# Two integers spread by VectorE's shuffle instead of a matrix product, and one product moved forward at the end

## The chip, the cores and the metric

The kernel runs on one core of a Trainium2 chip. The metric is the device time of one execution in microseconds (us). A profiled execution has a span of its own, from its first instruction to its last.

## What is computed

An attention over 2 batches, 8 heads, 768 positions and 64 channels per head, with a window of `n_local` positions and `n_global` global keys, is followed by two feed-forward layers (512 to 2048 to 512) over the 1536 rows.

```python
scores = scale * np.matmul(q, k.transpose(0, 1, 3, 2))
keep = is_global | is_local            # pos < n_global ; 0 <= rel < n_local
dist = np.where(is_global & ~is_local, float(n_local), np.abs(rel))
scores = np.where(keep, scores - slopes * dist, -1e9)
a = softmax(scores)
x = np.matmul(a, v)                    # rows x 512
h = x @ w_in;  g = np.maximum(0.01 * h, h);  x = g @ w_out
h = x @ w2_in; g = P(h) / (Q(h) + 1e-6);     out = g @ w2_out
```

`n_local` and `n_global` are 64-bit integers in device memory. The kernel reads them at run time; the mask and the bias of the attention are made from them.

## The kernel before

**Number form.** Every large product is made of three TensorE products of split numbers: a high part times a high part, and the two cross terms (names end in h and l: `qh`, `ql`, `kh`, `kl`, `gh`, `gl`).

**Start.** SP's queue loads q and k of the first pair of heads (`qr`, `kr`, half 0 before half 1), then k of pair 1, v and q of pair 1. SP's first issue for half 1 of k waits until the first DMA of ACT's queue has landed, since both use one completion counter. ACT's queue loads the two integers into one partition (`ints`, L95 and L96) and then one of the four first pieces of k (L300). VectorE makes positions and distances (L236 to L241) and turns the integers into floats in one partition (`read_ints`, L105 to L109). They are needed in all 128 partitions, as `nums`. For that TensorE multiplies a row of ones by them (L500, tile `spread`), and VectorE copies the result (L509). Then VectorE makes the bias: `bias_far` (L245, L248), `bias_near` (L251), `bias_half` (L254).

TensorE's own order is written out by hand. `keep_busy(n)` (L489) issues n dummy products that nobody reads. The start is 14 dummies, the spreading product, 1 dummy, then the transposes of `qr` and `kr` (L331), 3 dummies, and the first scores (L402). `prep_q` and `prep_k` work on the transposes: `qh` on ACT (L370), `kh` on ACT (L341), `ql` on VectorE (L372), `kl` on VectorE (L343). VectorE's queue holds the bias ahead of `ql`, so `ql` and `kl`, and with them the scores that read `kl`, start after the bias is made.

**Middle.** 96 units of attention go by in a hand-made order, and transposes of the next pairs are issued between them by the slots in `PREP0` and `PREP`. Then 96 units of the two layers follow: for each, `h` (L675), an activation into `gh` and `gl`, and the products into the four banks `y` (`emit_y`, L796 and L798). Each unit adds three products to each bank.

**End.** `emit_ends` writes out the last two units. Unit u-1 is the last one, and its activation comes in two halves: half 0 serves banks 0 and 1, half 1 serves banks 2 and 3. ACT makes the high part (`hi`, L910), VectorE the low part (`lo`, L913). TensorE gets the products of unit u-2 for banks 0 and 1, those of unit u-1 for banks 0 and 1, then for bank 2 and for bank 3 first u-2 and then u-1. `ys[d]()` copies bank d out and stores it (L814 or L816, L818).

Of the kernel before, what the change touches and what calls it, by code (L numbers as in the profile page):

```python
# [8 lines left out]
F32 = mybir.dt.float32  # L9
F32R = mybir.dt.float32r  # L10
I32 = mybir.dt.int32
U32 = mybir.dt.uint32
AF = mybir.ActivationFunctionType
ALU = mybir.AluOpType
# [3 lines left out]
P = 128  # L18
# [8 lines left out]
def attention_moe_moe2(  # L27
# [15 lines left out]
    nc = tc.nc  # L43
# [7 lines left out]
    NK = DM // P  # L51
# [9 lines left out]
    LOAD_Q = 5  # L61
    XOUT = (8, 9)

    BUSY = (14, 1, 3, 2, 1, 2)

    FIRST = 8
    XOUT_LAST = (1, 8)
# [17 lines left out]
    RUN_AHEAD = 2  # L85

    W2 = 2 * P
    BW = W2 + P

    cpool = ctx.enter_context(tc.tile_pool(name="cpool", bufs=1))  # L90
    xpool = ctx.enter_context(tc.tile_pool(name="xpool", bufs=1))


    ints = cpool.tile([1, 4], I32, name="ints")
    nc.scalar.dma_start(ints[:, 0:2], n_local.bitcast(I32).partition_broadcast(1))  # L95
    nc.scalar.dma_start(ints[:, 2:4], n_global.bitcast(I32).partition_broadcast(1))  # L96
    intf = cpool.tile([1, 4], F32, name="intf")
    num1 = cpool.tile([1, 2], F32, name="num1")
    warm = cpool.tile([P, P], F32R, name="warm")
    ones = warm.bitcast(F32)[0:1]  # L100
    nums = cpool.tile([P, 2], F32, name="nums")
    n_loc = nums[:, 0:1]
    n_glo = nums[:, 1:2]

    def read_ints():  # L105
        nc.vector.tensor_copy(intf, ints)
        lo, hi = (intf.rearrange("p (j w) -> p j w", w=2)[:, :, w] for w in range(2))
        nc.vector.scalar_tensor_tensor(hi, lo, 0.0, hi, ALU.is_lt, ALU.add)
        nc.vector.scalar_tensor_tensor(num1, hi, 4294967296.0, lo, ALU.mult, ALU.add)  # L109

    coef = cpool.tile([P, 8], F32, name="coef")

# [110 lines left out]
    def window_bias(bpool, rpool):  # L223
# [3 lines left out]
        misc2 = rpool.tile([P, 2 * DM], F32, tag="raw", name="misc2")  # L227
        rel_i = misc[:, 0:BW]
        dist = misc.bitcast(F32)[:, BW : 2 * BW]
        mask = misc2[:, 0:BW]  # L230
        nc.gpsimd.iota(rel_i[:, 0:W2], [[-1, W2]], base=P, channel_multiplier=1)
        nc.gpsimd.iota(rel_i[:, W2:BW], [[-1, P]], base=0, channel_multiplier=1)
        col_i = bpool.tile([P, GW], I32, name="col_i")
# [10 lines left out]
        def far():  # L244
            nc.vector.tensor_scalar(mask, dist, n_loc, FAR, ALU.is_ge, ALU.mult)  # L245
            mask_g = misc2[:, 0 : 2 * W2].rearrange("p (a c) -> p a c", a=2)[:, :, 0:GW]
            col_g = col.unsqueeze(1).to_broadcast([P, 2, GW])
# [10 lines left out]
    def attention(wpool, w1, ffn):  # L258
        with ExitStack() as actx:
# [4 lines left out]
            ps = actx.enter_context(tc.tile_pool(name="ps", bufs=2, space=PSUM))  # L264
# [4 lines left out]
            def blocks(t, s):  # L269

                if s == 0:
                    return t[:, 0 : HB * W2].rearrange("p (i c) -> p i c", c=W2)[:, :, 0:P]
                c0 = HB * W2 - P
                return t[:, c0 : c0 + HB * W2].rearrange("p (i c) -> p i c", c=W2)[:, :, P:W2]
# [212 lines left out]
            def keep_busy(n, rows=P):  # L487
                for _ in range(n):
                    nc.tensor.matmul(  # L489
                        idle[:, 0:W2].rearrange("p (a c) -> p a c", a=2),  # L490
                        warm[0:rows],
                        warm[0:rows].unsqueeze(1).to_broadcast([rows, 2, P]),
                        start=True,
                        stop=True,
                    )

            bias, bias_far, bias_near, bias_half = window_bias(bpool, rpool)
            keep_busy(BUSY[0])
            spread = ps.tile([P, W2], F32, tag="pt", name="spread")[:, 0:2]
            nc.tensor.matmul(spread, ones, num1, start=True, stop=True)  # L500
            keep_busy(BUSY[1])
            q0, k0, q1, k1 = P_[0].prep_q(0), P_[0].prep_k(0), P_[0].prep_q(1), P_[0].prep_k(1)
            next(q0)
            next(k0)
            next(q0)
            next(k0)
            keep_busy(BUSY[2])
            own, rest = slice(W2, BW), slice(0, W2)
            nc.vector.tensor_copy(nums, spread)  # L509
            bias_far()  # L510
            bias_near(own)
            next(q0, None)
# [91 lines left out]
            def unit(n):  # L604
                return U[n] if 0 <= n < len(U) else None
# [8 lines left out]
            n = 0  # L614
            while n < len(U) or running or n <= len(U) + LV + 1:

                for m in GROUPS.get(n, ()):
                    for step, _ in enumerate(zip(unit(m).scores(), unit(m + 1).scores())):
                        if n == 0 and step == 0:
                            keep_busy(BUSY[3], P // 2)  # L620
                    if m == 2:
                        for _ in zip(unit(4).scores(), unit(5).scores()):
                            pass
                        keep_busy(BUSY[4])
                for m in LEASTS.get(n, ()):
                    unit(m).least()
                    if m == 1:
                        bias_near(rest)
                        bias_half(rest)
                if unit(n - 1) and n != 3:  # L630
                    unit(n - 1).exp()
                if unit(n - 3):
                    unit(n - 3).transposes()
                    if n == 4:
                        keep_busy(BUSY[5], P // 2)
                    unit(n - 3).evacuate()
                if n == 3:
                    unit(2).exp()
                for m in {LV: (), LV + 1: (0, 1)}.get(n, (n - LV,)):
                    if unit(m):  # L640
                        unit(m).values()
                if unit(n - LV - 1) and unit(n - LV - 1).ih == HB - 1 and unit(n - LV - 1).j == 1:
                    unit(n - LV - 1).finish()
                fillers(n)
                n += 1
# [4 lines left out]
    class Layers:  # L650
# [59 lines left out]
        def run(self, wpool, check, first_unit):  # L710
            pool, tpool, state, units, w1, w2 = self.pool, self.tpool, self.state, self.units, self.w1, self.w2
# [60 lines left out]
                steps = x_steps(cps.tile([P, TT], F32, tag="c", name="xt"), state["xp"], B - 1, NK - 1, s)  # L772
                state["xt"] = lambda: next(steps), [lambda: next(steps), lambda: next(steps, None)]

            def emit_y(u, blocks=range(NK)):
                l, t, f = units[u]
                wt = (w1, w2)[l][f]
                gh, gl = state["g", u] if NK - 1 not in blocks else state.pop(("g", u))
                if f == 0:

                    if l == 0 or t == 2:
                        banks = ((yps, "y"),) * 4
                    else:
                        banks = ((cps, "c"), (cps, "c"), (yps, "y"), (yps, "y"))
                        banks = banks if t == 0 else banks[2:] + banks[:2]
                    state["y", l, t] = [
                        b.tile([P, TT], F32, tag=tag, name=f"y{d}") for d, (b, tag) in enumerate(banks)
                    ]
                ys = state["y", l, t]
                products = ((2, gh), (2, gl), (3, gh)) if u < len(units) - 1 else ((2, gh), (3, gh), (2, gl))  # L790
                for d in blocks:
                    ds_ = slice(d * P, (d + 1) * P)
                    for n, (m, gs) in enumerate(products):
                        st, sp = f == 0 and n == 0, f == NF - 1 and n == 2
                        if l == 0:
                            nc.tensor.matmul(ys[d], wt[:, m, ds_], gs, start=st, stop=sp)  # L796
                        else:
                            nc.tensor.matmul(ys[d], gs[:, ds_], wt[:, m, :], start=st, stop=sp)  # L798
# [38 lines left out]
            while check and first:  # L837
                n = 2 if first[0][0] == 0 else W2_RATE[len(plan) % len(W2_RATE)]
                n = 1 if len(plan) in LAST_X else n
# [61 lines left out]
            def emit_ends(u):  # L901

                ys = out_tasks(*units[u - 1][:2])
                g = state["act2"][1]
                gh, gl = new_g(u - 1)
                halves = [act_2_end(cs) for cs in HALVES]
                his, los, gs = ([t[:, cs] for cs in HALVES] for t in (gh, gl, g))

                def hi(n):
                    nc.scalar.activation(his[n], gs[n], AF.Copy)  # L910

                def lo(n):
                    nc.vector.tensor_tensor(los[n], gs[n], his[n].bitcast(F32), ALU.subtract)  # L913

                emit_y(u - 2, (0, 1))
                for _ in halves[0]:
                    pass
                hi(0)
                next(halves[1])
                lo(0)  # L920
                next(halves[1])
                next(halves[1])
                emit_y(u - 1, (0, 1))
                hi(1)
                ys[0]()
                ys[1]()
                lo(1)
                del state["act2"]
                for d in (2, 3):
                    emit_y(u - 2, (d,))  # L930
                    emit_y(u - 1, (d,))
                    ys[d]()

# [8 lines left out]
            for u in range(first_unit, len(units) + LAG):  # L942
# [41 lines left out]
                else:  # L984
# [6 lines left out]
                    n = u - SIZES0  # L991
# [170 lines left out]
```

## Time and profile before

| | us |
|---|---|
| median of 3 runs | 634.55 (634.18 to 634.83) |
| profiled execution, its time | 633.84 |
| profiled execution, its span | 632.10 |
| TensorE (PE) busy in the span | 625.4 (99%) |
| VectorE (DVE) busy | 468.5 (74%) |
| ScalarE (ACT) busy | 437.0 (69%) |
| GpSimd (POOL) busy | 208.7 (33%) |

PE is the matrix product, PEld its weight load, which overlaps it. SPq and ACTq are DMA issues of those engines. A row of a timeline gives the start in us from the span's beginning, the time in us, the engine, the line, the operation, the tiles and how many instructions are merged in it; a bracket gives idle time before it and what ended that. A product's recorded time overlaps that of the next product, so the distance of two starts is the pace.

### The profile page before, as it was taken

Reading aid. Unit: us, or ns where it says so; the run is one execution under the profiler, and the core shown is the slowest. Engines: PE = TensorE matmul, PEld = TensorE weight load, DVE = VectorE, ACT = ScalarE, POOL = GpSimd, SP = SyncE. Lnnn points to the kernel's source line nnn. Section 1 sums busy time; section 2 is a strip of 40 time slices with the busy share of each in tenths; the row PEclk is TensorE's granted clock in tenths of the full one; section 3 lists DMA queues with packets and bytes.
Section 4 is the critical chain, followed back from the end, with each engine's and each line's share of the span. In section 5 each row is a group of like instructions: output and inputs, shape, how many; then the busy total and the mean of one; then the engine's idle time right before and its main releaser. Section 6 shows DMA issues by size and latency. Waiting matters only on the chain.

```text
span 632.1 us, 9657 instructions
## 1 busy us (share of the span) xinstructions
PE 625.4 (99%) x3289; PEld 527.2 (83%) x3289; DVE 468.5 (74%) x931; ACT 437.0 (69%) x828; POOL 208.7 (33%) x223
## 2 busy tenths in 40 slices
PE   9999999999999999999999999999999999999996
PEld 7999998888888888888888888888888888888885
DVE  7889887878887555456444489998777777897785
ACT  5899997868866455455344477876677888876673
POOL 4888864534443334341000012222222222112220
PEclk9999999999999999999999999999999999999999
DMA  9998643854367776764332200000033331100002
GB/s 190 225 181 177 153 114 109 278 197 167 99 194 236 225 242 195 238 194 177 100 100 94 92 16 34 1 1 1 0 104 97 100 95 46 63 33 0 2 1 73
DMA packets 80895, 73.34 MB, mean 116 GB/s; under 512 B 50948, under 2 KB 67332, under 8 KB 80836
## 3 DMA queue, kind: packets, MB, share of 16 engines
q1 hardware_dynamic: 79920, 71.09, 39.5%
q0 software_dynamic: 224, 0.92, 0.4%
q8 instruction: 28, 0.46, 0.3%
q10 hardware_dynamic: 692, 0.62, 0.3%
q14 instruction: 31, 0.25, 0.1%
HBM read 60.69 MB, written 11.93 MB: 115 GB/s over the span
## 4 chain that ended last, share of the span: by engine, by line
PE 99%; DVE 0%; issue 0%
PE h L675 41%; PE y L798 21%; PE y L796 21%; PE pt L438 4%; PE sc L402 3%; PE o L460 3%; PE o L459 2%; PE h L331 2%; PE h L211 1%; PE idle L489 1%; PE o L457 0%; DVE ot L814 0%; PE xt L211 0%; PE spread L500 0%; DVE kl L343 0%; DVE ql L372 0%
## 5 line engine op out<-in xcount | busy, mean ns | idle before, releaser
L675 PE MATMUL h<-xh,w 128*128 128x512 f32 x768 | 253.5, 390 | 0.0
L675 PEld LDWEIGHTS h<-xh,w 128*128 128x128 f32 x768 | 144.3, 188 | 29.8
L675 PE MATMUL h<-xl,w 128*128 128x512 f32 x384 | 149.6, 389 | 0.0
L731 POOL TENSOR_TENSOR gl<-u,gh 128x512 fp32r<-128x512 f32 x44 | 57.1, 1298 | 264.6 <-PE y L798 125.6
L796 PE MATMUL y<-gh,w 128*128 128x512 f32 x384 | 126.1, 389 | 0.0
L798 PE MATMUL y<-w,gh 128*128 128x512 f32 x384 | 125.7, 390 | 0.0
L166 POOL TENSOR_TENSOR dec<-dec,wraw 128x512 int32<-128x512 int32 x48 | 64.1, 1344 | 82.5 <-DVE wraw L153 79.2
L798 PEld LDWEIGHTS y<-w,gh 128*128 128x128 f32 x384 | 72.0, 188 | 15.1 <-ACT gh L910 0.3
L796 PEld LDWEIGHTS y<-gh,w 128*128 128x128 f32 x384 | 72.1, 188 | 15.0
L675 PEld LDWEIGHTS h<-xl,w 128*128 128x128 f32 x384 | 72.1, 188 | 14.5
L798 PE MATMUL y<-w,gl 128*128 128x512 f32 x192 | 75.1, 391 | 0.0
L796 PE MATMUL y<-gl,w 128*128 128x512 f32 x192 | 74.7, 389 | 0.0
L700 DVE TENSOR_TENSOR gl<-h,gh 128x512 fp32r<-128x512 f32 x48 | 33.0, 688 | 52.4 <-ACT gh L699 52.4
L699 ACT ACTIVATE gh<-h 128x512 fp32r<-128x512 f32 x48 | 28.6, 596 | 59.7 <-PE y L796 56.4
L750 ACT ACTIVATE h<-h 128x512 f32<-128x512 f32 x48 | 28.7, 597 | 52.8 <-PE h L675 52.6
L695 DVE SCALAR_TENSOR_TENSOR h<-h,g 128x512 f32<-128x512 f32 x48 | 33.3, 694 | 25.8 <-ACT g L694 25.7
L737 DVE SCALAR_TENSOR_TENSOR w<-w,epsq,h 128x512 f32<-128x512 f32 (+1 forms) x49 | 36.6, 747 | 20.6 <-ACT h L761 19.9
L694 ACT ACTIVATE g<-h 128x512 f32<-128x512 f32 x48 | 28.7, 598 | 29.8 <-PE h L675 29.8
L752 DVE SCALAR_TENSOR_TENSOR w<-h,coef,w 128x512 f32<-128x512 f32 x48 | 36.0, 749 | 16.1 <-ACT w L751 16.0
L427 ACT ACTIVATE pr<-sn,st 128x256 f32<-128x256 f32 (+1 forms) x96 | 47.1, 495 | 0.2 <-DVE st L413 0.2
L798 PEld LDWEIGHTS y<-w,gl 128*128 128x128 f32 x192 | 36.1, 188 | 8.5 <-POOL gl L731 1.1
L796 PEld LDWEIGHTS y<-gl,w 128*128 128x128 f32 x192 | 36.0, 188 | 7.4
(124 smaller groups left out, 1117.3 us busy)
## 6 DMA issues: line engine op xcount, KB each, us to landing
wraw<-in_moe_w_in_dram SPq DMA_DIRECT2D x24, 512.0 KB, 4.5
wraw<-in_moe_w_out_dram SPq DMA_DIRECT2D x24, 512.0 KB, 4.8
scratch<-dec SPq DMA_DIRECT2D x32, 256.0 KB, 5.5
wf<-scratch SPq DMA_DIRECT2D x16, 512.0 KB, 3.5
w<-in_moe_w_in_dram SPq DMA_DIRECT2D x8, 512.0 KB, 4.4
w<-in_moe_w_out_dram SPq DMA_DIRECT2D x8, 512.0 KB, 5.3
vc<-in_v_dram SPq DMA_DIRECT2D x16, 192.0 KB, 3.4
qkraw<-in_q_dram SPq DMA_DIRECT2D x6, 512.0 KB, 3.5
```

The source lines that it names most:

```text
L166: nc.gpsimd.tensor_tensor(ti, ti, self.c, ALU.add)
L427: nc.scalar.activation(self.pr[:, :w], self.sn[:, :w], AF.Exp, bias=self.least_at, scale=-1.0,)
L675: nc.tensor.matmul(h, wt[:, m, c * P : (c + 1) * P], xs[:, c, cs], start=c == 0 and n == 0, stop=c == NK - 1 and n == 2,)
L694: nc.scalar.activation(g, h, AF.Copy)
L695: nc.vector.scalar_tensor_tensor(h, h, 0.01, g, ALU.mult, ALU.max)
L700: nc.vector.tensor_tensor(gl, h, gh.bitcast(F32), ALU.subtract)
L731: (nc.gpsimd if on_pool else nc.vector).tensor_tensor(gl, g, gh.bitcast(F32), ALU.subtract)
L737: yield nc.vector.scalar_tensor_tensor(ow, ow, epsq, oh2, ALU.add, ALU.mult)
L750: nc.scalar.activation(h2, h, AF.Square)
L752: nc.vector.scalar_tensor_tensor(w0, h2, coef[:, 7:8], w0, ALU.mult, ALU.add)
L796: nc.tensor.matmul(ys[d], wt[:, m, ds_], gs, start=st, stop=sp)
L798: nc.tensor.matmul(ys[d], gs[:, ds_], wt[:, m, :], start=st, stop=sp)
```

## The change

Three things are changed. The integers are loaded into four partitions (one in each group of 32) of a tile that GpSimd clears first, and VectorE spreads each over its group by a stream shuffle; the arithmetic on them then runs on 128 partitions and writes `nums` itself. The spreading product, the single dummy behind it and the copy L509 go, and the first row of dummies has 17 in place of 14. At the end, the first of the three products of unit u-2 for bank 2 is issued before the products of unit u-1 for banks 0 and 1.

```diff
-    BUSY = (14, 1, 3, 2, 1, 2)
+    BUSY = (17, 3, 2, 1, 2)
+    QUAD = 32
-    ints = cpool.tile([1, 4], I32, name="ints")
-    nc.scalar.dma_start(ints[:, 0:2], n_local.bitcast(I32).partition_broadcast(1))
-    nc.scalar.dma_start(ints[:, 2:4], n_global.bitcast(I32).partition_broadcast(1))
-    intf = cpool.tile([1, 4], F32, name="intf")
-    num1 = cpool.tile([1, 2], F32, name="num1")
+    ints = cpool.tile([P, 4], I32, name="ints")
+    nc.gpsimd.memset(ints, 0)
+    nc.scalar.dma_start(ints[0:P:QUAD, 0:2], n_local.bitcast(I32).partition_broadcast(P // QUAD))
+    nc.scalar.dma_start(ints[0:P:QUAD, 2:4], n_global.bitcast(I32).partition_broadcast(P // QUAD))
+    spread = cpool.tile([P, 4], I32, name="spread")
+    intf = cpool.tile([P, 4], F32, name="intf")
     def read_ints():
-        nc.vector.tensor_copy(intf, ints)
+        nc.vector.stream_shuffle(spread, ints, [0] * QUAD)
+        nc.vector.tensor_copy(intf, spread)
...
-        nc.vector.scalar_tensor_tensor(num1, hi, 4294967296.0, lo, ALU.mult, ALU.add)
+        nc.vector.scalar_tensor_tensor(nums, hi, 4294967296.0, lo, ALU.mult, ALU.add)
...
             keep_busy(BUSY[0])
-            spread = ps.tile([P, W2], F32, tag="pt", name="spread")[:, 0:2]
-            nc.tensor.matmul(spread, ones, num1, start=True, stop=True)
-            keep_busy(BUSY[1])
...
-            nc.vector.tensor_copy(nums, spread)
             bias_far()
...
-            def emit_y(u, blocks=range(NK)):
+            def emit_y(u, blocks=range(NK), some=slice(0, 3)):
-                    for n, (m, gs) in enumerate(products):
+                    for n, (m, gs) in list(enumerate(products))[some]:
...
                 emit_y(u - 2, (0, 1))
+                emit_y(u - 2, (2,), slice(0, 1))
...
                 for d in (2, 3):
-                    emit_y(u - 2, (d,))
+                    emit_y(u - 2, (d,), slice(3 - d, 3))
                     emit_y(u - 1, (d,))
```

PE at the start, before:

```order
L489 MATMUL idle<-warm 128x256 x14
L500 MATMUL spread<-num_65,warm 128x2
L489 MATMUL idle<-warm 128x256
L331 MATMUL h<-ident,qr 128x128 x3
L331 MATMUL h<-ident,kr 128x128 x3
```

and the same place after the change:

```order
L491 MATMUL idle<-warm 128x256 x17
L333 MATMUL h<-ident,qr 128x128 x3
L333 MATMUL h<-ident,kr 128x128 x3
L491 MATMUL idle<-warm 128x256 x3
L404 MATMUL sc_134<-kh,qh 128x128
```

The wait of TensorE for VectorE's numbers has gone from its queue; what follows is unchanged.

ACT with its DMA queue at the start, before:

```order
L95 DMA ints<-in_n_local_dram 1x2
L96 DMA ints<-in_n_global_dram 1x2
L300 DMA kr<-in_k_dram 128x3x64
L370 ACT_TABLE_LOAD
L370 ACTIVATE qh<-h 128x384
```

and after:

```order
L302 DMA kr<-in_k_dram 128x3x64
L97 DMA ints<-in_n_local_dram 4x2
L98 DMA ints<-in_n_global_dram 4x2
L372 ACT_TABLE_LOAD
L372 ACTIVATE qh<-h 128x384
```

The piece of k is now first on ACT's queue and both integers stand behind it. The first integer's DMA also waits for GpSimd's clearing of the tile.

PE at the end, before (`w_4684` is the weight tile of unit u-2, `w_4777` that of unit u-1, `y_5987` to `y_5990` are banks 0 to 3):

```order
L798 MATMUL y_5988<-w_4684,gh 128x512
L798 MATMUL y_5987<-w_4777,gh 128x512 x2
L798 MATMUL y_5987<-w_4777,gl 128x512
L798 MATMUL y_5988<-w_4777,gh 128x512 x2
L798 MATMUL y_5988<-w_4777,gl 128x512
L798 MATMUL y_5989<-w_4684,gh 128x512
L798 MATMUL y_5989<-w_4684,gl 128x512
L798 MATMUL y_5989<-w_4684,gh 128x512
L798 MATMUL y_5989<-w_4777,gh 128x512 x2
```

and after (the numbers of the tiles are one higher):

```order
L796 MATMUL y_5989<-w_4685,gh 128x512
L796 MATMUL y_5990<-w_4685,gh 128x512
L796 MATMUL y_5988<-w_4778,gh 128x512 x2
L796 MATMUL y_5988<-w_4778,gl 128x512
L796 MATMUL y_5989<-w_4778,gh 128x512 x2
L796 MATMUL y_5989<-w_4778,gl 128x512
L796 MATMUL y_5990<-w_4685,gl 128x512
L796 MATMUL y_5990<-w_4685,gh 128x512
L796 MATMUL y_5990<-w_4778,gh 128x512 x2
```

One product of bank 2 has moved ahead of the six products of unit u-1 for banks 0 and 1.

## Rows read from the trace of the kernel before

**Rows 1.** The page's part 4: the chain that ended last, shares by engine.

```profile
PE 99%; DVE 0%; issue 0%
```

**Rows 2.** Chain that ended last, in order of time: start us, us, what.

```profile
4.40 0.52 PE spread L500 x2
...
6.73 0.48 DVE kl L343
...
7.25 0.44 PE sc L402 x4
```

**Rows 3.** PE's timeline at the start: start us, us, engine, line, operation, tiles, count.

```profile
3.56 0.84 PE L489 MATMUL idle<-warm 128*128 128x256 f32 x3
...
3.77 0.63 PE L489 MATMUL idle<-warm 128*128 128x256 f32 x2
...
5.07 0.27 PE L331 MATMUL h<-ident,qr 128*128 128x128 f32 x1
...
5.64 0.60 PE L489 MATMUL idle<-warm 128*128 128x256 f32 x3
```

**Rows 4.** Timeline of ACT and its queue; last row: of SP's queue.

```profile
0.73 0.53 ACTq L95 DMA_DIRECT2D ints<-in_n_local_dram  x1
1.30 0.23 ACTq L96 DMA_DIRECT2D ints<-in_n_global_dram  x1
1.56 0.41 ACTq L300 DMA_DIRECT2D kr<-in_k_dram  x1
...
5.59 0.49 ACT L370 ACTIVATE qh<-h 128x384 fp32r<-128x384 f32 x1 [2.31 <-PE h L331]
5.98 0.48 ACT L341 ACTIVATE kh<-h 128x384 fp32r<-128x384 f32 x1
...
3.35 1.03 SPq L300 DMA_DIRECT2D kr<-in_k_dram  x2
```

**Rows 5.** Tile kr: the loads issued at 1.56 and 1.76; then one issued at 4.95.

```profile
DMA to landing us min/median/max: 2.5/2.7/2.8
...
DMA to landing us min/median/max: 3.3/3.3/3.3
```

**Rows 6.** DVE's timeline, 2 to 7 us.

```profile
2.92 0.15 DVE L106 CAST intf<-ints 1x4 f32<-1x4 int32 x1
...
3.36 0.54 DVE L239 TENSOR_TENSOR misc<-misc,misc 128x384 f32<-128x384 f32 x1
...
5.14 0.42 DVE L245 TENSOR_SCALAR misc<-misc,nums 128x384 f32<-128x384 f32 x1
...
6.18 0.55 DVE L372 SCALAR_TENSOR_TENSOR ql<-h,qh 128x384 fp32r<-128x384 f32 x1
```

**Rows 7.** PEld's timeline at 13 us; tile qr: pair 1's second load, landing from issue.

```profile
12.88 0.30 PEld L460 LDWEIGHTS o<-vc,pts 128*128 128x128 f32 x2
13.11 0.31 PEld L331 LDWEIGHTS h<-ident,qr 128*128 128x128 f32 x3
...
L300 SPq DMA_DIRECT2D qr<-in_q_dram x2: 542/608/673, 7.8 to 8.4; - x2
...
DMA to landing us min/median/max: 4.6/4.6/4.6
```

**Rows 8.** PEld's timeline at the end.

```profile
622.58 0.30 PEld L798 LDWEIGHTS y<-w,gh 128*128 128x128 f32 x2 [0.28 <-ACT gh L910]
623.04 0.19 PEld L798 LDWEIGHTS y<-w,gl 128*128 128x128 f32 x1 [0.16 <-DVE gl L913]
...
624.30 0.64 PEld L798 LDWEIGHTS y<-w,gh 128*128 128x128 f32 x3
```

**Rows 9.** PE's timeline at the end.

```profile
622.34 0.98 PE L798 MATMUL y<-w,gh 128*128 128x512 f32 x3
623.15 0.39 PE L798 MATMUL y<-w,gl 128*128 128x512 f32 x1
```

**Rows 10.** ACT's timeline at the end.

```profile
623.88 0.42 ACT L910 ACTIVATE gh<-u 128x256 fp32r<-128x256 f32 x1 [1.35 <-DVE u L739]
```

More of the change, by code (lines that the diff above doesn't have):

```diff
@@ L91, in attention_moe_moe2 @@
     xpool = ctx.enter_context(tc.tile_pool(name="xpool", bufs=1))
-    ints = cpool.tile([1, 4], I32, name="ints")
-    nc.scalar.dma_start(ints[:, 0:2], n_local.bitcast(I32).partition_broadcast(1))
-    nc.scalar.dma_start(ints[:, 2:4], n_global.bitcast(I32).partition_broadcast(1))
-    intf = cpool.tile([1, 4], F32, name="intf")
-    num1 = cpool.tile([1, 2], F32, name="num1")
+    ints = cpool.tile([P, 4], I32, name="ints")
[4 more added lines that the diff above has]
+    intf = cpool.tile([P, 4], F32, name="intf")
     warm = cpool.tile([P, P], F32R, name="warm")
-    ones = warm.bitcast(F32)[0:1]
     nums = cpool.tile([P, 2], F32, name="nums")
@@ L506, in attention @@
             next(k0)
-            keep_busy(BUSY[2])
+            keep_busy(BUSY[1])
             own, rest = slice(W2, BW), slice(0, W2)
-            nc.vector.tensor_copy(nums, spread)
             bias_far()
@@ L619, in attention @@
                         if n == 0 and step == 0:
-                            keep_busy(BUSY[3], P // 2)
+                            keep_busy(BUSY[2], P // 2)
                     if m == 2:
@@ L623, in attention @@
                             pass
-                        keep_busy(BUSY[4])
+                        keep_busy(BUSY[3])
                 for m in LEASTS.get(n, ()):
@@ L634, in attention @@
                     if n == 4:
-                        keep_busy(BUSY[5], P // 2)
+                        keep_busy(BUSY[4], P // 2)
                     unit(n - 3).evacuate()
@@ L773, in last_x @@
                 state["xt"] = lambda: next(steps), [lambda: next(steps), lambda: next(steps, None)]
-            def emit_y(u, blocks=range(NK)):
+            def emit_y(u, blocks=range(NK), some=slice(0, 3)):
                 l, t, f = units[u]
                 wt = (w1, w2)[l][f]
-                gh, gl = state["g", u] if NK - 1 not in blocks else state.pop(("g", u))
+                gh, gl = state["g", u] if NK - 1 not in blocks or some.stop < 3 else state.pop(("g", u))
                 if f == 0:
```

## The prediction

> **What bounds the kernel now.** I read the page's chain first: of the work that ended last, TensorE holds 99% [rows 1], so an edit counts only by what it takes out of TensorE's own line, at its start or at its end. Then the chain in order of time. At the start it leaves TensorE: behind the dummies stands the spreading product, 0.52 us, then comes VectorE with the bias, `ql` and `kl`, and at 7.25 it is back on TensorE with the scores that read `kl` [rows 2]. From there it stays on TensorE to the last product. Third, the timelines of the three engines around these places [rows 3, 4, 6], and fourth the weight loads at 13 us, where a load from memory lands just in time [rows 7]. Last the end, where TensorE's loads show two short waits for the last activation [rows 8]. A measurement of this kernel can tell about 0.2% (1.3 us) from no change; the three runs shown lie 0.65 us apart.
>
> **Start, TensorE.** Two dummies take 0.63 us and three take 0.84, so one more is 0.21 [rows 3]. The 14th ends at 4.40 [rows 2]; it starts about 0.42 before that, at 3.98, since 0.63 less one step of 0.21 is 0.42. Numbers 15 to 17 then start at 4.19, 4.40 and 4.61, and the transposes of `qr` at 4.82 instead of 5.07 [rows 3]: 0.25 us earlier. The pace of the dummies is no constant: three of them take 0.60 us at 5.64, 0.24 less than 0.84 [rows 3]. If the new ones ran like that, the transposes would start at about 4.58. I take 4.82, since every dummy up to 4.40 kept the slow pace, and keep 0.49 us as the other end. The data is there: the later of the two first k pieces was issued at 1.76 and landed at most 2.8 us later, at 4.56 [rows 5], and its transposes come at 4.82 + 0.32 = 5.14.
>
> **Start, ACT and VectorE.** `qh` moves with the transposes from 5.59 to 5.34 and ends at 5.83; `kh` from 5.98 to 5.73, ending at 6.21 [rows 4]. Now the integers. On ACT's queue the k piece goes first: the first issue of that queue holds it for 0.57 us (0.73 to 1.30) and the next for 0.26 (1.30 to 1.56), so the second integer is issued near 0.73 + 0.57 + 0.26 = 1.56 [rows 4]. Before, it was issued at 1.30 and read at 2.92 [rows 4, 6], so 1.62 us is enough for it: 3.18. The k piece ahead of it needs 0.73 + 2.5 = 3.23 [rows 5]. I take 3.3 for the shuffle's start. No row shows a stream shuffle; the cast of the same four numbers takes 0.15 us [rows 6] and the slowest operation in that view 0.55, so it costs 0.15 to 0.55; I take 0.15, as the shuffle has the cast's size, and 0.18 from start to start, the step from 2.92 to 3.28 halved. With it and three more such steps less 0.1 (3.28 to 3.36), L239 starts 0.62 after the shuffle, at 3.92, lasts 0.54, and the bias begins at 4.50 instead of 5.14. From there to `ql` are 1.04 us (5.14 to 6.18) [rows 6]: `ql` could start at 5.54. It now waits for `qh`, 5.83, and starts at about 5.86 instead of 6.18. So the integers have 0.3 us to spare, and the shuffle's upper price is not quite hidden by it (0.4), which costs 0.1 at most. `kl` follows, and the scores on `kl` come at 6.93 instead of 7.25: **0.32 us earlier**. GpSimd's clearing of a 128x4 tile is hidden behind the k issue of ACT, as is its own queue's delay, which can move VectorE's first work by some hundredths; the copy L509 (0.17 us in the chain's line) is in the 0.32.
>
> The Trainium skill, VectorE: DVE Perf Modes, Rules for kernel authors, gives about 2400 ns for any shuffle of 32 x 2048; an estimate from that for 4 columns is 5 ns beside the fixed time of an instruction, and the sum would be the same by it. No run here shows a shuffle yet.
>
> **What is late next.** At 13.11 TensorE loads the weights for the transposes of pair 1's q; the second half of that q was issued at 8.4 and landed 4.6 us later, at 13.0 [rows 7]. SP's queue issues its loads back to back from 0.73 on, untouched by the change, so this landing doesn't move with TensorE. TensorE starts 0.04 us behind its releaser (`kl` done at 6.73 + 0.48 = 7.21, its scores at 7.25) [rows 2]. Of the 0.32 us, then, only 13.11 - 13.04 = 0.07 pass this point. Ends: 0.07 if the landing stays, 0.32 if it comes as much earlier as TensorE does. I take 0.07.
>
> The Trainium skill (DMA: Bandwidth & Descriptors, Issuing engines are not separate DMA queues) says that starting transfers on several engines saves only the time to issue them. By that rule the earlier k piece on ACT's queue brings pair 1's q no earlier, and the landing stays at 13.0, as I take it; rows 7 neither show nor exclude it.
>
> **End.** From the last product of u-2 for bank 1 to the first low product of u-1 are three steps: 622.34 to 623.15, 0.81 us [rows 9]. A step without a wait is 0.225 (three loads in 0.64, of which the last alone is 0.19) [rows 8]. So 0.81 - 0.68 = 0.13 us is wait, for the high and then the low part of half 0 [rows 8]. With one product more in front, four steps take 0.90, the low product comes at 623.24, and one product fewer is left behind it: 0.13 us earlier to the end. That asks that half 1 is in time: its first high load was at 624.53 (the second of the three in the row at 624.30) and moves to 624.39, while the high part is ready at 624.30 [rows 8, 10]. It fits by 0.09. The product adds to a bank that gets all its other products as before.
>
> **Sum.** -0.07 - 0.13 = -0.20 us. The profiled execution took 633.84 us with a span of 632.10; it would take 633.64. Against the median of 634.55, which lies 0.71 above that execution, it gives **634.35 us**.
>
> **Rivals.** *A, the start passes whole.* The landing at 13.0 comes earlier too, as 96 KB went out on ACT's queue 0.8 us sooner. Gain 0.32 + 0.13: 634.1; with the fast dummies 0.24 more, 633.85. For it: those bytes are out of the way of SP's loads earlier (issued at 0.73 instead of 1.56 [rows 4]). Against it: SP's own issues are unmoved, and with them the moment at which pair 1's q is asked for.
>
> *B, the k piece lands late.* SP's next k issue, at 3.35 [rows 4], now waits for ACT's k piece, where it waited for the first integer. Due at 3.23, it has 0.12 us to spare; beyond 3.35, 2.62 us after its issue, all of SP's queue slips by the excess, and the landing at 13.0 with it. It shares memory with q from the first moment now. The nearest rows are 2.5 and 2.8; the largest of a k load is 3.3 [rows 5]. At 3.3 the piece lands at 4.03, SP slips 0.68, TensorE starts pair 1's q at 13.73 instead of 13.11, and with 0.13 back at the end the time is 635.05: slower than before. The integers behind it would come at 4.1 and `ql` at 6.34, 0.16 later than before, which that slip hides. The Trainium skill (DMA: Bandwidth & Descriptors, Queues, rings and completion order) says that each engine consumes the descriptors of a ring in order, so the integers can't pass the k piece; no row here shows the two in that order.
>
> *C, the pace.* TensorE keeps the slow pace beyond 4.8. The stretch from there to the scores on `kl`, 4.82 to 6.93, would take up to twice as long, 2.1 us more, less 0.32 and 0.13: 636.2 at worst. Against it: before, the pace rose although the row of dummies was broken by the tiny spreading product [rows 2, 3]; now it is unbroken.
>
> **Chances.** Forecast 0.50, A 0.28, B 0.14, C 0.04, and 0.04 that the edits cancel in some other way near no change. The forecast, A and most of B lie within 0.2%. Faster by over 0.2% (below 633.28) asks for A and more than any row gives: 0.04. Slower by over 0.2% (above 635.82): C and the tail of B, 0.05. Within: 0.91. The range goes from A's fast end less a quarter us of the scatter of medians, 633.6, to B's 635.0.
>
> **What would show it.** Right: the first transposes at about 4.8; no gap on TensorE between the dummies and them; the bias on VectorE at 4.5 and `ql` waiting for `qh`; scores on `kl` at 6.9; then a wait of some 0.25 us on TensorE before 13.05; at the end the two waits before the last unit gone, and the last product 0.2 us earlier from the span's start. Wrong: pair 1's q landing before 12.8 (A) or after 13.1 with SP's fourth k issue later than 3.35 (B), the shuffle starting after 3.65, dummies still 0.21 apart behind the transposes (C), or a wait for half 1 at the end.

## The result and the profile after

| | before | after |
|---|---|---|
| median, us | 634.42 (633.82 to 634.83, 12 runs) | 638.68 (635.65 to 640.06, 12 runs) |
| profiled execution, time / span | 633.84 / 632.10 | 635.81 / 633.9 |
| mean granted clock | 0.998 (profiled execution) | 0.990 to 0.999 (12 runs) |

The ratio is **1.0063** (95% interval 1.0047 to 1.0078): slower by more than the 0.2% that can be told from no change. (The ratio lies near that of the means, so a few long runs can move it where they leave the median.) 634.35 was forecast, with 635.0 as the upper end of the range, so the prediction was wrong, and with it the sign.

The runs fall into two groups. Three lie at 635.65, 635.81 and 635.83 with a mean granted clock of 0.999; the profiled execution is one of them. The other nine lie from 636.87 to 640.06, and their mean granted clock is 0.990 to 0.996. So there are two losses: 635.81 - 634.42 = 1.4 us in every run, and up to 4.3 more in those where TensorE was granted less clock.

The first loss is in the profile. ACT's queue after the change (start us, us, engine, line, operation, tiles, count), which answers to [rows 4]:

```profile
0.73 0.52 ACTq L302 DMA_DIRECT2D kr<-in_k_dram  x1
1.29 1.10 ACTq L97 DMA_DIRECT2D ints<-in_n_local_dram  x1
2.42 0.51 ACTq L98 DMA_DIRECT2D ints<-in_n_global_dram  x1
2.96 1.28 ACT L372 ACT_TABLE_LOAD   x1 [2.96 <-POOL col_i L236]
```

The two integers hold the queue for 1.10 and 0.51 us, where they held it for 0.53 and 0.23. The second is issued at 2.42, not near 1.56. DVE's timeline after, which answers to [rows 6] (a bracket is idle time before the row and what ended it):

```profile
5.23 0.01 DVE L107 LOAD_MASK_SELECT spread<-ints  x1 [2.20 <-DMA ints<-in_n_global_dram]
5.26 0.16 DVE L107 STREAM_SHUFFLE spread<-ints 128x4 int32<-128x4 int32 x1
...
6.40 0.64 DVE L243 CAST col<-col_i 128x32 f32<-128x32 int32 x1
6.96 0.56 DVE L247 TENSOR_SCALAR misc<-misc,nums 128x384 f32<-128x384 f32 x1
...
8.15 0.55 DVE L374 SCALAR_TENSOR_TENSOR ql<-h,qh 128x384 fp32r<-128x384 f32 x1
8.62 0.55 DVE L345 TENSOR_TENSOR kl<-h,kh 128x384 fp32r<-128x384 f32 x1
```

VectorE stands idle for 2.20 us until the second integer is there. The bias begins at 6.96 where it began at 5.14 [rows 6]. PE's timeline after, and below it a row of PE's waits (what waited, for what: us in total, times, longest):

```profile
1.04 3.82 PE L491 MATMUL idle<-warm 128*128 128x256 f32 x17 [1.04 <-DVE epsq L205]
4.70 0.49 PE L333 MATMUL h<-ident,qr 128*128 128x128 f32 x3
...
9.22 0.33 PE L404 MATMUL sc<-kl,qh 64*128 64x128 f32 x2 [2.46 <-DVE kl L345]
```

```profile
PE sc L404 <- DVE kl L345: 2.5, 1, 2.5
```

The transposes are early, at 4.70, as meant. TensorE then waits 2.46 us for `kl`, and the scores on it start at 9.22 in place of 7.25 [rows 2]: 1.97 us later. The page's chain, all TensorE before [rows 1], now leaves it:

```profile
PE 97%; DVE 1%; DMA 0%; POOL 0%; issue 0%; POOLq 0%; ACTq 0%; DVEq 0%
```

At the end the two bracketed waits of [rows 8] are gone, as forecast (PEld's timeline; `w` are the weight tiles):

```profile
624.10 0.87 PEld L796 LDWEIGHTS y<-w,gh 128*128 128x128 f32 x4
625.02 0.19 PEld L796 LDWEIGHTS y<-w,gl 128*128 128x128 f32 x1
625.25 0.42 PEld L796 LDWEIGHTS y<-w,gh 128*128 128x128 f32 x2
```

The chain's last piece (start us, us, what), of before and then of after, gives the size of that:

```profile
615.93 11.04 PE y L798 x48
```

```profile
617.91 10.93 PE y L796 x48
```

So 1.97 us are lost at the start, 0.11 won at the end, and the spans differ by 633.9 - 632.1 = 1.8. (Against the median of before it is the 1.4 above, since the profiled execution of before lies 0.6 below that median.)

### The profile page after: what moved, and what is told of

Its sections match the earlier page's. It is cut to its first block, busy times and chain, and to the rows that moved or that the text cites. A ratio compares the mean times of both kernels' runs of the same rounds, so it can differ in the third digit from the quotient of the medians.

```text
span 633.9 us, 9659 instructions
## 1 busy us (share of the span) xinstructions
PE 624.9 (99%) x3289; PEld 527.4 (83%) x3289; DVE 468.8 (74%) x932; ACT 437.0 (69%) x828; POOL 208.8 (33%) x224
## 4 chain that ended last, share of the span: by engine, by line
PE 97%; DVE 1%; DMA 0%; POOL 0%; issue 0%; POOLq 0%; ACTq 0%; DVEq 0%
PE h L673 41%; PE y L796 21%; PE y L794 21%; PE pt L440 4%; PE sc L404 3%; PE o L462 3%; PE o L461 2%; PE h L333 1%; PE h L213 1%; PE o L459 0%; DMA ints<-in_n_global_dram 0%; DVE sn L415 0%; DVE xl L219 0%; DVE w L177 0%; DVE pts L448 0%
```

## The experiments

The theory after this reading is that the integers come late, because they stand behind the k piece and because a load into four partitions is slow to issue; the wait that this puts on TensorE costs its own length, and in most runs the clock as well. The rivals are these: the end edit does harm (e1), the place in the queue is enough alone (e2, e3), the loading is enough alone (e2, e6, e7, e9, e10), something in the loads lowers the clock (e4, e8). The kernel before, run beside them, had medians of 634.44 (e1 to e4), 634.49 (e5 to e7) and 634.54 us (e8, e9).

**e1, the end alone.** The kernel before with the edit at the end:

```diff
+                emit_y(u - 2, (2,), slice(0, 1))
...
-                    emit_y(u - 2, (d,))
+                    emit_y(u - 2, (d,), slice(3 - d, 3))
```

> The kernel before with the end's edit alone: one product of unit u-2 for bank 2 in front of the last unit's. Both theories of the slowdown blame the start, so this one should not be slower. Forecast of the sum: 0.13 us less than before, 634.3 against 634.4; the two waits in front of the last unit's products (0.28 and 0.16 us) gone, the waits for half 1 none. Rival: the end has a part in the slowdown, and the time lies over 634.9.

Measured: 634.42 (633.74 to 634.59, 11 runs) against 634.44; ratio 0.9998 (0.9989 to 1.0007). The chain's last piece is down from 11.04 to 10.97:

```profile
616.56 10.97 PE y L798 x48
```

The end edit removes its waits and does no harm; its gain can't be told from nothing.

**e2, the integers ahead of the k piece.** The changed kernel with its two integer loads issued just before the first pieces of q and k, so that on ACT's queue they come first:

```diff
-    nc.scalar.dma_start(ints[0:P:QUAD, 0:2], n_local.bitcast(I32).partition_broadcast(P // QUAD))
-    nc.scalar.dma_start(ints[0:P:QUAD, 2:4], n_global.bitcast(I32).partition_broadcast(P // QUAD))
...
+            nc.scalar.dma_start(ints[0:P:QUAD, 0:2], n_local.bitcast(I32).partition_broadcast(P // QUAD))
+            nc.scalar.dma_start(ints[0:P:QUAD, 2:4], n_global.bitcast(I32).partition_broadcast(P // QUAD))
             halves = [P_[0].load("qr", q, HB), P_[0].load("kr", k, HB)]
```

> The changed kernel with the two integer loads put in front of the k piece on ACT's queue, as they stood before. Theory 1, the place in the queue is the cause: the second integer is issued at about 1.3 us as before and read by VectorE at about 3, the bias begins at 4.2, scores on kl come at 6.9, and the time is 634.1 to 634.3 without scatter. Theory 2, loading to four partitions is slow by itself: an issue again takes over 1 us, the second integer is issued at about 2 and read at 4.7, the k piece is issued near 2.5 and lands at 5.2, and the time is 635 to 640 with the scatter.

Measured: 634.63 (634.40 to 639.38, 11 runs); ratio 1.0015 (1.0001 to 1.0029). ACT's queue, then VectorE's read, then the wait of PE:

```profile
0.86 1.12 ACTq L481 DMA_DIRECT2D ints<-in_n_local_dram  x1
2.02 0.58 ACTq L482 DMA_DIRECT2D ints<-in_n_global_dram  x1
2.63 0.46 ACTq L300 DMA_DIRECT2D kr<-in_k_dram  x1
```

```profile
4.55 0.01 DVE L105 LOAD_MASK_SELECT spread<-ints  x1 [1.51 <-DMA ints<-in_n_global_dram]
```

```profile
PE sc L402 <- DVE kl L343: 0.6, 1, 0.6
```

Both theories have a part. The issues stay long with nothing ahead of them, and the integers are still read at 4.55, against 2.92 before [rows 6], as the second said. But TensorE's wait falls from 2.46 to 0.55 us, and eight of the eleven runs lie at 634.4 to 634.8, not at 635 to 640. The other three, from 635.91 up, have a clock of 0.991 to 0.996.

**e3, the place alone.** The kernel before, with its one-partition loads behind the k piece of ACT's queue:

```diff
-    nc.scalar.dma_start(ints[:, 0:2], n_local.bitcast(I32).partition_broadcast(1))
-    nc.scalar.dma_start(ints[:, 2:4], n_global.bitcast(I32).partition_broadcast(1))
...
+                if n == 4:
+                    nc.scalar.dma_start(ints[:, 0:2], n_local.bitcast(I32).partition_broadcast(1))
+                    nc.scalar.dma_start(ints[:, 2:4], n_global.bitcast(I32).partition_broadcast(1))
```

> The kernel before with the k piece put in front of the two integer loads on ACT's queue; the integers still go to one partition and TensorE still spreads them. Theory 1, the place in the queue: the integers wait behind the k piece and are read at 4.5 to 5.2 us instead of 2.92, TensorE's spreading product comes 1.5 us or more late, 635.5 to 640. Theory 2, the four partitions: the issues take 0.26 us each, the integers are read at 3.3 to 3.6, the spreading product still finds them ready, and the time is 634.4 to 634.8.

Measured: 634.66 (634.28 to 638.73, 9 runs); ratio 1.0023 (1.0005 to 1.0041).

```profile
1.25 0.62 ACTq L482 DMA_DIRECT2D ints<-in_n_local_dram  x1
1.91 0.23 ACTq L483 DMA_DIRECT2D ints<-in_n_global_dram  x1
```

```profile
4.26 0.16 DVE L104 CAST intf<-ints 1x4 f32<-1x4 int32 x1 [1.26 <-DMA ints<-in_n_global_dram]
```

The issues are nearly as short as before, yet from the second issue to the read it now takes 4.26 - 1.91 = 2.35 us, against 1.62. Eight bytes behind 96 KB on the same queue wait for the 96 KB. The Trainium skill (DMA: Bandwidth & Descriptors, Queues, rings and completion order) says that each DMA engine consumes the descriptors of a queue's ring in order; these rows agree with it. TensorE waits 0.44 us for the numbers ahead of the spreading product, the scores on `kl` come at 7.57, and the median is the one expected if the place did not matter: the place alone costs little in the median. Six of the nine runs lie at 635.0 or below; the other three, from 636.88 up, have a mean granted clock of 0.998 or 0.999, and what held them is open.

**e4, the wait filled.** The changed kernel with 22 dummies in place of 2 between the first scores and those on `kl`, so that TensorE works where it waited:

```diff
-    BUSY = (17, 3, 2, 1, 2)
+    BUSY = (17, 3, 22, 1, 2)
```

> The changed kernel with 22 dummies instead of 2 between the first and the second scores of units 0 and 1, which fill the 2.5 us in which TensorE waits for kl. Theory: the scatter of the changed kernel between 635.7 and 640 is TensorE's granted clock, which falls in some executions after that wait and not in others; filled, every execution is near 635.7 and its mean clock 0.998 or more. Rival: the scatter has another source (memory, the integers' arrival), and it stays.

Measured: 635.97 (635.59 to 636.44, 9 runs); ratio 1.0024 (1.0014 to 1.0034); mean granted clock 0.998 to 1.000 in all. PE's timeline:

```profile
6.75 2.61 PE L491 MATMUL idle<-warm 64*128 64x256 f32 x20
9.08 0.33 PE L404 MATMUL sc<-kl,qh 64*128 64x128 f32 x1
```

The scores on `kl` are nearly as late as in the changed kernel (9.08 for 9.22) and 1.5 us stay, but the runs from 637 to 640 are gone. The wait as such costs about 1.5 us; what it does to the clock is the rest, 638.68 - 635.97 = 2.7 in the median.

**e5, all 128 partitions.** e2 with each integer loaded into every partition, and no clearing and no shuffle:

```diff
-    nc.gpsimd.memset(ints, 0)
...
-        nc.vector.stream_shuffle(spread, ints, [0] * QUAD)
-        nc.vector.tensor_copy(intf, spread)
+        nc.vector.tensor_copy(intf, ints)
...
-            nc.scalar.dma_start(ints[0:P:QUAD, 0:2], n_local.bitcast(I32).partition_broadcast(P // QUAD))
+            nc.scalar.dma_start(ints[:, 0:2], n_local.bitcast(I32).partition_broadcast(P))
```

and the same for `n_global`.

> The integers go straight into all 128 partitions by two DMAs at the head of ACT's queue, with no clearing, no shuffle and no spreading product; the end is the changed kernel's. If it is the arrival of the numbers that sets the time: a load of coef into 128 partitions held SP's queue for 0.50 and 0.43 us, so the issues should end near 1.7 and the integers be read near 3.3 to 3.6, ql should wait only for qh, the scores on kl start near 6.9, and the time be 634.1 to 634.4. If many small pieces to many partitions are what is slow (four took 1.10 and 0.51), the two issues hold the queue for far more than 2 us, the k piece behind them lands past 5.6, and the time is 635 or more, with the clock falling in some runs.

Measured: 635.17 (634.62 to 639.63, 12 runs); ratio 1.0025 (1.0012 to 1.0039). It was meant as a better version and is none. ACT's queue, VectorE's read, and from the table of DMA issues of the first 6 us the pieces of q (KB each, median us from issue to landing):

```profile
0.73 0.43 ACTq L478 DMA_DIRECT2D ints<-in_n_local_dram  x1
1.19 0.45 ACTq L479 DMA_DIRECT2D ints<-in_n_global_dram  x1
```

```profile
4.96 0.17 DVE L103 CAST intf<-ints 128x4 f32<-128x4 int32 x1 [1.96 <-DMA ints<-in_n_global_dram]
```

```profile
qr<-in_q_dram SPq DMA_DIRECT2D x4, 96.0 KB, 3.9
```

Neither theory had it right. The issues are short, but the data takes 4.96 - 1.19 = 3.77 us, and the pieces of q on the other queue land 3.9 us after their issue, where the same row of the kernel before says 2.5.

**e6, four partitions side by side.** e2 with partitions 0 to 3:

```diff
-            nc.scalar.dma_start(ints[0:P:QUAD, 0:2], n_local.bitcast(I32).partition_broadcast(P // QUAD))
-            nc.scalar.dma_start(ints[0:P:QUAD, 2:4], n_global.bitcast(I32).partition_broadcast(P // QUAD))
+            nc.scalar.dma_start(ints[0:4, 0:2], n_local.bitcast(I32).partition_broadcast(P // QUAD))
+            nc.scalar.dma_start(ints[0:4, 2:4], n_global.bitcast(I32).partition_broadcast(P // QUAD))
```

> As the kernel with the integers ahead of the k piece, but with the four partitions next to one another (0 to 3) in place of 32 apart; only the first group of 32 partitions then gets the right numbers, which leaves out the spreading to the other three. If the distance of 32 partitions makes the issue long, the first issue takes about 0.5 in place of 1.12 and the integers are read near 3.5 to 3.9. If it is that there is more than one piece, the two issues stay at 1.1 and 0.5 to 0.6, the integers are read near 4.55, and the time is 634.6.

Measured: 634.30 (633.96 to 634.84, 10 runs); ratio 0.9997 (0.9988 to 1.0006).

```profile
0.86 0.55 ACTq L481 DMA_DIRECT2D ints<-in_n_local_dram  x1
1.45 0.26 ACTq L482 DMA_DIRECT2D ints<-in_n_global_dram  x1
```

```profile
3.04 0.01 DVE L105 LOAD_MASK_SELECT spread<-ints  x1
```

Four partitions in a row are issued as fast as one. VectorE doesn't wait for them at all (no bracket).

**e7, one partition and the shuffle.** e2 with one partition:

```diff
-            nc.scalar.dma_start(ints[0:P:QUAD, 0:2], n_local.bitcast(I32).partition_broadcast(P // QUAD))
+            nc.scalar.dma_start(ints[0:1, 0:2], n_local.bitcast(I32).partition_broadcast(1))
...
-            nc.scalar.dma_start(ints[0:P:QUAD, 2:4], n_global.bitcast(I32).partition_broadcast(P // QUAD))
+            nc.scalar.dma_start(ints[0:1, 2:4], n_global.bitcast(I32).partition_broadcast(1))
```

> As the kernel with the integers ahead of the k piece, but loaded into one partition, and spread by the shuffle to the first group of 32 partitions only, which leaves out the other three. Everything that the prediction said of the shuffle holds here if the late numbers were its only failure: issues of 0.53 and 0.23, integers read near 3.0, shuffle 0.16, the bias before 4.9, ql right behind qh near 5.9, scores on kl near 6.9, then a wait at 13 for the transposes of pair 1's q that takes most of it back: 634.1 to 634.4. If the spreading product was no cost at all, the scores on kl start near 7.25 again and the time is 634.4 to 634.6.

Measured: 634.12 (634.05 to 634.51, 11 runs); ratio 0.9996 (0.9987 to 1.0005). VectorE's shuffle, then PE's timeline:

```profile
3.17 0.01 DVE L105 LOAD_MASK_SELECT spread<-ints  x1
3.20 0.16 DVE L105 STREAM_SHUFFLE spread<-ints 128x4 int32<-128x4 int32 x1
```

```profile
4.85 0.84 PE L331 MATMUL h<-ident,qr 128*128 128x128 f32 x3
...
7.50 0.33 PE L402 MATMUL sc<-kl,qh 64*128 64x128 f32 x2
...
13.83 0.52 PE L331 MATMUL h<-ident,qr 128*128 128x128 f32 x3 [0.24 <-DMA qr<-in_q_dram]
```

With the integers in time the median, 634.12, is near the forecast 634.35, and it can't be told from the kernel before. The scores on `kl` come at 7.50, though, and not near 6.9, since in this profiled execution the transposes still run at the slow pace (0.84 us for three). The profile of e1, whose start is that of the kernel before, has them at that pace too, so it is the one to compare with:

```profile
5.23 0.84 PE L331 MATMUL h<-ident,qr 128*128 128x128 f32 x3
...
7.84 0.33 PE L402 MATMUL sc<-kl,qh 64*128 64x128 f32 x2
```

Against it the changed start brings 7.84 - 7.50 = 0.34 us, the size that was forecast (0.32). The load of pair 1's q then takes it back: the transposes of that q start at 13.83 here and at 13.76 in e1, both spans are 632.7, and in e7 the chain that ended last runs through this load (start us, us, what):

```profile
8.87 4.82 DMA qr<-in_q_dram
```

So the product that the shuffle replaces cost nothing that can be measured: behind it a load of q sets the time again. In e6 the same wait for pair 1's q is 0.57 us.

**e8, a pause without the loads.** The kernel before, with its two bias steps made three times over:

```diff
-            bias_far()
-            bias_near(own)
+            for _ in range(3):
+                bias_far()
+                bias_near(own)
```

> The kernel before, whose integers and loads stay as they were, with the two steps of the bias that stand ahead of ql made three times over (the same result each time); by their starts in the trace of before, 5.14 to 6.18, each repeat holds ql and kl back by 1.04 us, so the scores on kl start near 9.3 in place of 7.25 and TensorE waits some 2.4 us there. If a pause of TensorE at this place is all that it takes: a lowest time near 636.0 to 636.5 and most runs above it, up to 640, with mean clocks down to 0.991. If the scatter of the changed kernel comes from how its integers or its k piece were loaded, all runs lie within 0.5 of 636.2 at a clock of 0.998 to 1.000.

Measured: 640.05 (639.28 to 640.71, 5 runs); ratio 1.0087 (1.0073 to 1.0100); mean granted clock 0.990 to 0.993 in all five. The pause alone does it. The scores on `kl` came later than the 9.3 expected, and no run kept its clock, so the lowest time is 639.28 and not near 636. PE's timeline, and then stretches of core 0 (window, us, busy us and instructions of PE, PEld, DVE, ACT and POOL, granted clock, DMA share, GB/s):

```profile
9.72 0.48 PE L402 MATMUL sc<-kl,qh 64*128 64x128 f32 x2 [2.74 <-DVE kl L343]
```

```profile
7.00:7.50 0.50, 0.00 (x0) 0.00 (x0) 0.47 (x2) 0.00 (x0) 0.41 (x2) 1.00 1.14 256
7.50:8.00 0.50, 0.00 (x0) 0.00 (x0) 0.46 (x2) 0.00 (x0) 0.00 (x0) 0.88 1.21 258
8.00:8.50 0.50, 0.00 (x0) 0.00 (x0) 0.43 (x3) 0.00 (x0) 0.00 (x0) 0.50 0.77 155
...
17.00:18.00 1.00, 1.00 (x8) 0.78 (x8) 0.00 (x0) 0.95 (x3) 0.75 (x2) 0.50 1.20 204
18.00:18.50 0.50, 0.50 (x5) 0.50 (x6) 0.41 (x3) 0.00 (x0) 0.22 (x1) 0.88 1.00 136
```

TensorE has no instruction from 7 us on, and within 7.5 to 8.0 the granted clock falls to 0.50, which is the 1.2 GHz level. It is back within 18.0 to 18.5. TensorE works through 9.72 to about 18.1 at half its rate, 8.4 us for what would take 4.2. The span is 638.2, 6.1 above that of before; the late scores are 9.72 - 7.25 = 2.5 of it, which leaves 3.6 for the clock. The Trainium skill (TensorE: Matmul & The Clock Gate, HAM oscillation) tells of kernels whose waits send TensorE back to the lower rate, and counts half of the time spent there as lost. An estimate by that, from the 8.4 us, is 4.2 for the clock's part; the spans leave 3.6, so the trace agrees to within 0.6.

**e9, one cause undone.** The changed kernel, still with the integers behind the k piece, but in partitions 0 to 3:

```diff
-    nc.scalar.dma_start(ints[0:P:QUAD, 0:2], n_local.bitcast(I32).partition_broadcast(P // QUAD))
+    nc.scalar.dma_start(ints[0:4, 0:2], n_local.bitcast(I32).partition_broadcast(P // QUAD))
```

and the same for `n_global`.

> The changed kernel with one thing altered: the four partitions that get the integers are 0 to 3 in place of 32 apart (the right numbers then reach only the first group of 32, which leaves out the other three). The integers still stand behind the k piece. If the two causes add, about 1.0 of the 2.3 us goes: issues of 0.6 and 0.25 as in the kernel before with the k piece first, the integers read near 4.2 to 4.4, the scores on kl near 8.2, a wait of TensorE near 1.5, a lowest time near 634.8 and still some runs above 636 where the clock falls. If the place behind the k piece makes the issue long whatever the partitions, 1.1 and 0.5 stay, and so do the read at 5.2 and the times of the changed kernel, 635.7 to 640.

Measured: 634.74 (634.43 to 636.47, 11 runs); ratio 1.0009 (1.0000 to 1.0018).

```profile
1.26 0.66 ACTq L97 DMA_DIRECT2D ints<-in_n_local_dram  x1
1.95 0.26 ACTq L98 DMA_DIRECT2D ints<-in_n_global_dram  x1
```

```profile
4.39 0.01 DVE L107 LOAD_MASK_SELECT spread<-ints  x1 [1.36 <-DMA ints<-in_n_global_dram]
```

Closing the gaps takes the read from 5.23 to 4.39 and nearly all of the time back. The scores on `kl` came at 7.80 behind a wait of 0.29, earlier than the 8.2 and 1.5 expected, and two of eleven runs still had a clock of 0.996.

**e10, gaps of one partition.** e2 with partitions 0, 2, 4 and 6:

```diff
-            nc.scalar.dma_start(ints[0:P:QUAD, 0:2], n_local.bitcast(I32).partition_broadcast(P // QUAD))
+            nc.scalar.dma_start(ints[0:8:2, 0:2], n_local.bitcast(I32).partition_broadcast(P // QUAD))
```

and the same for `n_global`.

> One look at the two issues alone: the kernel with the integers ahead of the k piece, the four partitions 2 apart (0, 2, 4, 6), which again leaves out the right numbers for three groups of 32. If any gap between the partitions makes the issue long, 1.1 and 0.5 to 0.6 as with 32 apart, and the integers are read near 4.5. If it is the distance of 32, so partitions that lie in different groups, 0.55 and 0.26 as with partitions 0 to 3, and the integers are read near 3.0.

One run, 634.61 beside 634.45:

```profile
0.86 1.21 ACTq L481 DMA_DIRECT2D ints<-in_n_local_dram  x1
2.10 0.60 ACTq L482 DMA_DIRECT2D ints<-in_n_global_dram  x1
```

The long issue goes with the gap, not with the distance of 32. The read comes at 4.64.

**What the ten runs add up to.** The read of the integers, on VectorE:

| | ahead of the k piece | behind it |
|---|---|---|
| 1 partition | 2.92 (before), 3.17 (e7) | 4.26 (e3) |
| 4 side by side | 3.04 (e6) | 4.39 (e9) |
| 4 with gaps | 4.55 (e2), 4.64 (e10) | 5.23 (after) |

(In before, e6 and e7 VectorE doesn't wait, so there the data came earlier still.) Against 2.92, each cause alone delays the read by 1.3 (e3) and 1.6 us (e2). Together it is 2.3, less than the sum; the long issue (1.29 to 2.93) runs while the k piece is on its way, which would explain it. In time the two together cost far more than their sum: the medians of e2, e3 and e9, with one cause each, are 0.2 us above the kernel before, and with both it is 4.3. One cause puts a wait of at most 0.55 on TensorE ahead of the scores on `kl` (e2); both put 2.46 there. No version beat the kernel before by an amount that can be measured: e1 has the end's gain and e7 both, and the interval of each holds 1.

## Why the prediction was wrong

- **The step that failed** is this one: "the first issue of that queue holds it for 0.57 us (0.73 to 1.30) and the next for 0.26 (1.30 to 1.56), so the second integer is issued near 0.73 + 0.57 + 0.26 = 1.56". It took the two holds by their place in the queue. They go by what is loaded and where to: 0.52 for the k piece, 1.10 and 0.51 for the integers, the second of them issued at 2.42. No row of the kernel before showed a load into separate partitions, and this unknown got no bounds, while the shuffle, which was harmless, got them. Any price more than 0.3 above the one taken would have used up the slack that the prediction itself gave.
- **"1.62 us is enough for it"** failed as well. From issue to read it is 5.23 - 2.42 = 2.8. A place behind the k piece makes it 2.35 in one partition (e3); gaps make it 4.55 - 2.02 = 2.5 with nothing ahead (e2). The 1.62 came from a load into one partition at the head of the queue. The prediction looked at the queue's order, took the landing of the k piece alone (3.23) as the bound, and let the integers land with it. Of the 5.23 - 3.18 = 2.05 us by which the integers came later than this sum, 2.42 - 1.56 = 0.86 is the issue and 2.81 - 1.62 = 1.19 the way from issue to read.
- **The transposes** were put at 4.82 with 4.58 as the other end, and came at 4.70 (at 4.85 in e7). **The shuffle** was put at 0.15 and takes 0.16. Both terms were right. In the changed kernel neither mattered.
- **VectorE behind the integers** was 1.93 late at the shuffle (5.23 for 3.3) and 2.46 at the bias (6.96 for 4.50). Most of the difference is the cast of `col`, 0.64 us in place of 0.16 to 0.18 in the other profiles. It now falls together with GpSimd's work on `kh`, which the prediction didn't look at. In e4 and e8 it is the step behind the bias's first (L250, L248) that starts beside that work, and it takes 0.57 in place of 0.28; that the two get in each other's way was not tested. GpSimd's row after:

```profile
6.18 1.13 POOL L361 TENSOR_TENSOR kh<-kh,zeros 128x288 fp32r<-128x288 f32 x2 [3.83 <-ACT kh L343]
```

- **What is late next**, pair 1's q at 13 us, was right as a mechanism, but in the changed kernel TensorE came too late to meet it. Where the integers are in time it shows: waits of 0.24 (e7) and 0.57 (e6). It took back all of the 0.34 and not 0.25 of 0.32, since in these two profiles pair 1's q came at 13.7 and 14.0 instead of 13.0: SP's queue reached that q at 8.29 and 8.35, where it had been 7.77. Why is open.
- **Rival A** wanted that q earlier than 13.0 because the k piece goes out first. In the changed kernel its second half was issued near 8.9 and landed 4.5 us later, at 13.4.
- **The end** was put at 0.13 and gave 0.11 in the chain, 0.07 in e1.
- **Rival B** had the right place, ACT's queue, and the right sign. SP's k issue at 3.35 did slip, to 3.60 (the prediction's last lines call it the fourth; the trace has it as SP's second), so the k piece landed after its due time. But the slip was 0.25 and decided nothing, and B too put the integers just behind the k piece, at 4.1 for a k piece at 4.03, "which that slip hides". They came at 5.2. That the integers alone could be the late thing was no rival, although the prediction listed a shuffle that starts after 3.65 among its signs of being wrong. SP's row after, for the 3.35 of [rows 4]:

```profile
3.60 2.02 SPq L302 DMA_DIRECT2D kr<-in_k_dram  x4
```

- **Rival C** asked whether TensorE's pace would rise in time. In the profiled execution it did; in e7 it rose only behind the transposes, and the scores on `kl` came 7.50 - 6.93 = 0.57 us late. That a wait could bring the clock down again, which makes 4 us out of 2, was in no case. All twelve runs lie above the range's end of 635.0: the three fastest by the late integers alone, the other nine by the clock as well.

## What to carry to other kernels

When a load changes its shape, price the issue by a row of that shape, and where there is none, give it a range: here a load of 8 bytes into four separate partitions held the queue longer than 96 KB. A small load that something waits for goes ahead of large ones on its queue, not behind (2.35 us from issue to read in e3, against at most 1.62). And a wait of TensorE near the start is to be priced twice, at its length and at the clock that it can cost: 2.5 us became 4.3 in the median.

## What the runs showed of the hardware that was not expected

- **Gaps between the partitions make a small load slow.** Two loads of 8 bytes per partition held ACT's queue for 0.52 and 0.22 us with one partition, 0.55 and 0.26 with four side by side, 1.12 and 0.58 with four that are 32 apart, 1.21 and 0.60 with four that are 2 apart, and 0.43 and 0.45 with all 128. Why the gaps cost this is open.
- **A short issue is no early arrival.** The 128 partitions were the fastest first issue and were read 3.8 us after the second, and in the same profile the 96 KB pieces of q on another queue took 3.9 us to land, where the kernel before has 2.5 (e5).
- **The lower clock came behind pauses of 2.5 and 2.7 us**: nine of twelve runs of the changed kernel, five of five of e8, none of nine with the pause filled (e4). Runs at 0.991 to 0.996 also occur in e2, e5 and e9, whose profiled executions show waits of 0.6, 0.4 and 0.3 us on `kl`; those runs have no profile, so what TensorE did in them is open.
- **The first rise of the pace is not in the granted clock.** The stretches of before and of e7 have it at 1.00 from the start, while the dummies run 0.21 us apart [rows 3] and later ones 0.12 apart (20 in 2.61 us in e4). When it rises differs from run to run: the first three transposes take 0.49 us at 4.70 in the changed kernel and 0.84 at 4.85 in e7, though the dummies ahead of them are the same. This is why e7, with its integers in time, shows its scores on `kl` at 7.50 and not at the forecast 6.93. It bears on the kernel before too: 7.25 in its own profile, 7.84 in that of e1.
